# Forgetting attention with an MLP behind it: batch 1's loads issued in another order, five banks for the first scores, a bank of its own for the last pair's second head

## The chip, the cores and the metric

The kernel runs on one core of one Trainium2 chip. The metric is the time that the device takes for one execution, in microseconds (us), as the median of several runs; lower is better. A profile of one execution gives a trace. Its span runs from the first to the last instruction, and the execution's own time is a little longer than the span.

The core's engines work side by side, each through its own list of instructions in order: TensorE (PE: matmuls, and PEld for the loads of its weights), VectorE (DVE), ScalarE (ACT), GpSimd (POOL) and SyncE (SP). They wait for each other through semaphores. GpSimd and SyncE also issue DMAs, the transfers between the device's memory and the core; all of GpSimd's go through one queue.

## What is computed

There are 8 batches with 8 heads, 576 positions and 64 values per head. For each head, with `cum` the running sum of log f:

```python
scores = scale * np.matmul(q, k.transpose(0, 1, 3, 2))
log_f = np.log(np.clip(f, 0.0001, 1.0))
cum = np.cumsum(log_f, axis=-1)
decay = cum[:, :, :, None] - cum[:, :, None, :]
scores = np.where(causal, -1000000000.0, scores + decay)
attn = np.exp(scores - max) / (sum + 1e-09)
x = np.matmul(attn, v)
h = x @ w_in
out = (h - np.tanh(h)) @ w_out
```

The result of the attention, with the heads of a position side by side, is 4608 rows of 512 values. Each goes through an MLP with 2048 hidden values. Inputs and output are fp32; the kernel loads q, k, v and the weights as fp16.

## The kernel before

**Pairs.** The attention is done for two heads at a time: 32 pairs, four to a batch. Pairs are numbered from 0, so pairs 0 to 3 are batch 0 and pair 4 is the first of batch 1 (`NPAIR` is 4). For a pair, q and k are turned on TensorE into `QT` and `KT` (`trans`, two copies by VectorE or ScalarE each; from batch 3 on, transposing DMAs do this). Then come seven score tiles (`scores`, tiles 0 to 6; tile 3 holds the short last blocks of both heads). Each is a product into a PSUM bank, an exponential on ScalarE into a tile `e` (or `el`), and a causal mask. For pairs 0 to 3 (`early`) the mask is a small extra product on TensorE; from pair 4 on GpSimd cuts `e` (line 311). The pair's `values` multiply e with v, one pair later, and VectorE divides by the row sums into `xn`. `turn` transposes xn into `XR`, the MLP's input: on TensorE for batch 0, by two DMAs of SyncE for later ones.

**The decay** is added through three extra rows of QT and KT, filled by DMAs of SyncE from `cc` and `cqs`. These hold `cum`, which comes from a clip (line 160), a logarithm on ScalarE and a scan on VectorE. The very first head takes the decay by extra products instead, so that it need not wait for those DMAs.

**The MLP** works on nine blocks of 512 rows. A block has 16 steps `mlp1` (one 128-wide piece of the hidden layer each: four matmuls into `hps`, tanh `th` on ScalarE, sum `gt` on VectorE) and 16 steps `mlp2` (four matmuls each; every fourth ends a product `ops`, copied out and stored). `mlp1_part` does the first three matmuls of a step ahead ("h0" to "h2"), before the last pair of batch 0 is turned.

**What sets the order.** The program is written in the order in which each engine runs it. For pairs 0 to 4 `ORDERS` is a list by hand: "s" a score tile, "q" and "k" turns of a pair, "va" and "vb" the values of the two heads of the pair before, "x" its `turn`, "m" the next MLP step, "h" a part step, "r" rows and pads for the second buffers, and a number so many idle matmuls (`spin`) on a spare bank. From pair 5 on, a fixed count of MLP steps (`take`: 5 up to pair 8, then 8) is spread over each pair's items; so a step's place depends on how many are done before. `LOADS` says behind which score tile of which pair a load is issued: `(3, 3)` is behind pair 3's tile 3. Loads and masks share GpSimd's list, so a load behind a mask is issued when that mask is done, and a mask behind a load waits for the load to be issued.

**Banks.** PSUM has eight banks: two for scores (`ps_sc`), two for the values of a pair (`ps_av`, one for each head), one for turns (`ps_tr`), three for the MLP (`ps_m`; before the MLP starts, the turns of pairs 0 to 3 use them).

Of the kernel before, what the change touches and what calls it, by code (L numbers as in the profile page):

```python
# [14 lines left out]
PITCH = 640  # L15
# [7 lines left out]
def kernel(  # L23
# [111 lines left out]
    def load_aug(b, h0=0):  # L135
# [19 lines left out]
    nc.vector.memset(QT[0][D:D + 3, 0, :], 0.0)  # L155
    nc.vector.memset(KT[0][0:D, :, S:PITCH], 0.0)
    nc.vector.memset(KT[0][D:D + 3, 1:H, S:PITCH], 0.0)
    nc.vector.memset(neg16, 0.0)
    nc.vector.memset(tri16, 0.0)
    nc.vector.tensor_scalar(out=lf, in0=lf, scalar1=0.0001, scalar2=1.0,  # L160
                            op0=ALU.max, op1=ALU.min)
# [9 lines left out]
    nc.vector.memset(vn[0][D:P, NJ - 1, :, :], 0.0)  # L171
    nc.vector.memset(vn[0][:, :, :, D:VW], 1.0)
# [16 lines left out]

    def later_rows():  # L190
# [10 lines left out]
    def load_wout(t0, t1):  # L201
# [3 lines left out]
    QW = DFF // 4  # L205
    LOADS = {(0, 3): [lambda: load_win(0, QW), lambda: load_win(QW, 2 * QW)],
             (1, 3): [lambda: load_win(2 * QW, 3 * QW), lambda: load_win(3 * QW, DFF)],
             (2, 3): [lambda: load_qk(qn, q, 1, 0, 2), lambda: load_qk(kn, k, 1, 0, 2)],
             (3, 3): [lambda: load_wout(0, NFT // 2), lambda: load_qk(qn, q, 1, 2, 4),
                      lambda: load_qk(kn, k, 1, 2, 4), lambda: load_wout(NFT // 2, NFT)],  # L210
             (NPAIR, 1): [lambda: load_v(1)],
             (NPAIR, 4): [lambda: load_qk(qn, q, 1, 4, H), lambda: load_qk(kn, k, 1, 4, H),
                          lambda: const_rows(0, 0, 1)],
             (NPAIR, 6): [lambda: load_qk(qn, q, 2, 0, H), lambda: load_qk(kn, k, 2, 0, H)]}
# [18 lines left out]
    E, XN, AV, HP, GT, M2 = {}, {}, {}, {}, {}, {}  # L233

# [5 lines left out]
    def trans(b, c, src, dst, early, engs):  # L240
        pn, g3 = S // NT6, NT6 // 2
        if early:
            t32 = ps_m.tile([P, UW], FP32, tag="m", name="t32")
        else:
            t32 = ps_tr.tile([P, UW], FP32, tag="tr", name="t32")
        t16 = t32.bitcast(FP16)[:, 0:2 * S // 2].rearrange("p (a g n) -> p a g n", a=2, g=g3)
        for a in range(2):
            for g in range(g3):
                nc.tensor.transpose(out=t16[:, a, g, :], in_=src[b % 2][:, 2 * c + a, 2 * g:2 * g + 2, :],  # L249
                                    identity=id16[0:pn, 0:pn])  # L250
# [23 lines left out]
    def scores(b, c, ti, early):  # L274
        ps = ps_sc.tile([P, 512], FP32, tag="sc", name="ps")
# [38 lines left out]
    def values(b, c, heads=(0, 1), apart=False):  # L314
        if 0 in heads:
            av = ps_av.tile([P, 2, 512], FP32, tag="av", name="av")
            AV[(b, c)] = av[:, :, 0:NJ * (D + 1)].rearrange("p a (i d) -> p a i d", i=NJ)
        av = AV[(b, c)]
        for a in heads:
            for ib in range(NJ):  # L320
                for j in range(ib + 1):
                    nc.tensor.matmul(out=av[:, a, ib, :], lhsT=E.pop((b, c, a, j, ib)),  # L322
                                     rhs=vn[b % 2][:, j, 2 * c + a, 0:D + 1],
                                     start=(j == 0), stop=(j == ib))
        h0, hn = (heads[0], 1) if apart else (0, 2)
        if not apart and 1 not in heads:
            return
        if (b, c) not in XN:
# [3 lines left out]
        nc.vector.tensor_scalar_add(out=rs, in0=av[:, h0:h0 + hn, :, D:D + 1], scalar1=1e-9)  # L332
        nc.vector.reciprocal(out=rs, in_=rs)
        nc.vector.tensor_tensor(out=xn[:, :, h0 * D:(h0 + hn) * D].rearrange("p i (a d) -> p a i d", a=hn),  # L334
                                in0=av[:, h0:h0 + hn, :, 0:D],
# [17 lines left out]
    def mlp1_part(u, ft, c0, c1):  # L353
        if c0 == 0:
            HP[(u, ft)] = ps_m.tile([P, UW], FP32, tag="m", name="hps")
# [19 lines left out]
    def mlp2(u, s):  # L375
# [7 lines left out]
        if part == 3:  # L383
# [7 lines left out]
    BEGIN = ["8", "q0", "k0", "3", "s0", "q1", "s1", "k1", "s2", "s4", "s5", "q2", "r", "s6", "s3"]  # L391
    ORDERS = [BEGIN,
# [5 lines left out]

    def att_items(p):
# [12 lines left out]
        if p <= NPAIR:  # L412
            for what in ORDERS[p]:
# [6 lines left out]
                elif kind in "qk":  # L420
                    put(trans, *pairs[p + int(arg)], *((qn, QT) if kind == "q" else (kn, KT)), early,
# [5 lines left out]
                elif kind == "r":  # L427
                    put(later_rows)
                elif kind == "x":
# [75 lines left out]
```

## Time and profile before

| | |
|---|---|
| median of the timed runs | 369.54 us (369.54, 368.87, 371.0) |
| the profiled execution | 368.07 us |
| its span | 366.4 us |
| TensorE busy | 346.3 us, 95% |
| ScalarE busy | 219.2 us, 60% |
| VectorE busy | 183.1 us, 50% |
| GpSimd busy | 162.7 us, 44% |
| GpSimd's DMA queue | 18.36 MB, 75.3% of 16 engines' span |

The page cuts the span into 40 slices and gives each engine's busy share in tenths, and the clock that TensorE was granted. The other views are: the waits, summed by who waited for whom; the chain of work that ended last; the instructions in order of time (start, length, engine, line, operation, what it writes and reads; in brackets the idle time ahead of it and what ended it); and tables by stretches. In these the columns are the stretch, its length, the busy time and count of TensorE, PEld, VectorE, ScalarE and GpSimd, the granted clock, the DMA share and GB/s.

### The profile page before, as it was taken

The page shows a single profiled execution, that of the slowest core. Times are in us where ns is not written, and L with a number is a line of the kernel's source. Part 1 is how long each engine was busy: PE and PEld are TensorE (multiplying, and loading weights), DVE is VectorE, ACT ScalarE, POOL GpSimd, SP SyncE. Part 2 cuts the span into 40 slices and gives each one's busy share as a digit, 9 for nine tenths or more (in the row PEclk, how much of TensorE's full clock was granted, in tenths as well). Part 3 has the DMA queues.
Part 4 walks back from the last instruction along what each step waited for, and adds up shares of the span by engine and source line. Part 5 has one row for each costly group of instructions (what it writes and reads, how often), then busy time and mean ns, then how long its engine had stood idle before and what let it go on. Part 6 is the DMA issues. An engine that isn't in the chain of part 4 may idle for free.

```text
span 366.4 us, 7488 instructions
## 1 busy us (share of the span) xinstructions
PE 346.3 (95%) x2787; PEld 189.6 (52%) x2787; DVE 183.1 (50%) x358; ACT 219.2 (60%) x413; POOL 162.7 (44%) x318
## 2 busy tenths in 40 slices
PE   5986839999999999999999999999999999999995
PEld 2663415565555555555556875555555554444442
DVE  7564745445882278327832683278227622812710
ACT  5674644657865686568756875687568733623621
POOL 8950195587546754765476537662222210000000
PEclk9899997999999999999999999999999999999999
DMA  9999999999949994999399969994220022012002
GB/s 102 129 191 192 139 105 152 123 137 163 119 79 140 133 168 61 142 149 150 68 139 135 151 84 139 137 152 85 73 75 16 18 75 73 1 40 76 0 33 83
DMA packets 164819, 38.73 MB, mean 106 GB/s; under 512 B 155779, under 2 KB 160111, under 8 KB 164783
## 3 DMA queue, kind: packets, MB, share of 16 engines
q0 software_dynamic: 116480, 18.36, 75.3%
q1 hardware_dynamic: 48302, 19.90, 27.2%
q8 instruction: 22, 0.36, 0.4%
q14 instruction: 15, 0.11, 0.1%
HBM read 36.85 MB, written 9.44 MB: 126 GB/s over the span
## 4 chain that ended last, share of the span: by engine, by line
PE 89%; DVE 3%; ACT 2%; DMA 2%; POOL 1%; issue 1%; ACTq 0%
PE ops L381 33%; PE hps L363 33%; PE ps L287 12%; PE av L322 8%; ACT e L301 1%; DMA qn<-in_q_dram 1%; PE t L249 1%; DMA XR<-xn 1%; POOL vn L106 1%; DVE xn L334 1%; ACT th L370 1%; PE ps L295 0%; DVE gt L373 0%; DVE cum L173 0%; PE ps L290 0%
## 5 line engine op out<-in xcount | busy, mean ns | idle before, releaser
L373 DVE TENSOR_TENSOR gt<-hps,th 128x512 f16<-128x512 f32 x144 | 99.4, 691 | 92.8 <-ACT th L370 91.9
L363 PE MATMUL hps<-XR,win 128*128 128x512 f16 (+1 forms) x640 | 141.0, 359 | 1.7 <-DVE gt L373 1.0
L381 PE MATMUL ops<-wout,gt 128*128 128x512 f16 x576 | 139.1, 379 | 0.0
L301 ACT ACTIVATE e<-ps 128x512 f16<-128x512 f32 x192 | 110.4, 594 | 37.3 <-PE ps L287 31.1
L311 POOL TENSOR_SCALAR_AFFINE_SELECT e<-e 128x128 f16<-128x128 f16 x168 | 56.8, 340 | 125.0 <-ACT e L301 124.4
L370 ACT ACTIVATE th<-hps 128x512 f32<-128x512 f32 x144 | 86.1, 599 | 39.0 <-PE hps L363 38.2
L363 PEld LDWEIGHTS <-win 128*128 128x128 f16 x640 | 58.2, 98 | 50.7 <-issue 3.2
L287 PE MATMUL ps<-QT,KT 67*128 67x64 f16 (+4 forms) x384 | 78.6, 279 | 3.6 <-DVE KT L260 1.8
L381 PEld LDWEIGHTS <-gt 128*128 128x128 f16 x576 | 51.9, 97 | 52.4
L385 ACT ACTIVATE ost<-ops 128x512 f32<-128x512 f32 x36 | 21.5, 597 | 63.4 <-PE ops L381 49.1
L287 PEld LDWEIGHTS <-KT 67*128 67x128 f16 x384 | 36.8, 98 | 39.2 <-issue 4.2
L322 PEld LDWEIGHTS <-e 128*128 128x128 f16 x896 | 33.2, 98 | 8.0 <-issue 1.6
L322 PE MATMUL av<-vn,e 128*128 128x65 f16 x896 | 34.7, 194 | 1.0 <-DVE xn L334 1.0
L332 DVE TENSOR_SCALAR rs<-av 128x10 f32<-128x10 f32 (+1 forms) x33 | 5.4, 164 | 49.7 <-PE av L322 49.3
L106 POOL DMA_DIRECT2D vn<-in_v_dram x32 | 28.7, 899 | 3.0 <-PE hps L363 1.2
L334 DVE TENSOR_TENSOR xn<-av,rs 128x640 f16<-128x640 f32 (+1 forms) x33 | 26.6, 805 | 1.1
L87 POOL DMA_DIRECT2D qn<-in_q_dram x25 | 22.2, 889 | 1.3 <-issue 0.8
L87 POOL DMA_DIRECT2D kn<-in_k_dram x25 | 21.4, 857 | 1.3 <-issue 1.1
L260 DVE COPY QT<-t 64x576 f16<-64x576 f16 x22 | 9.9, 452 | 13.6 <-PE t L249 13.5
L260 DVE COPY KT<-t 64x576 f16<-64x576 f16 (+1 forms) x26 | 11.2, 429 | 4.3 <-PE t L249 4.1
L322 PE MATMUL av<-vn,el 128*128 128x65 f16 x64 | 12.4, 195 | 0.0
L249 PE MATMUL t<-id,qn 96*128 96x96 f16 x72 | 5.8, 224 | 5.8 <-DMA qn<-in_q_dram 5.8
(62 smaller groups left out, 134.6 us busy)
## 6 DMA issues: line engine op xcount, KB each, us to landing
out_dram<-ost SPq DMA_DIRECT2D x36, 256.0 KB
vn<-in_v_dram POOLq DMA_DIRECT2D x32, 128.0 KB, 4.9
qn<-in_q_dram POOLq DMA_DIRECT2D x20, 128.0 KB, 4.7
kn<-in_k_dram POOLq DMA_DIRECT2D x20, 128.0 KB, 4.4
win<-in_moe_w_in_dram POOLq DMA_DIRECT2D x4, 512.0 KB, 10.7
wout<-in_moe_w_out_dram POOLq DMA_DIRECT2D x2, 1024.0 KB, 18.9
XR<-xn SPq DMA_TRANSPOSE x56
qn<-in_q_dram POOLq DMA_DIRECT2D x6, 144.0 KB, 4.4
```

The costliest lines, as they stand in the source:

```text
L87: nc.gpsimd.dma_start(out=dst[b % 2][0:pn, n, :].rearrange("p (h d) -> p h d", h=H), in_=src[b, :, n * P:n * P + pn, :].rearrange("h p d - ...
L106: nc.gpsimd.dma_start(out=vn[b % 2][:, n, h0:h1, 0:D], in_=v[b, h0:h1, n * P:(n + 1) * P, :].rearrange("h p d -> p h d"))
L287: nc.tensor.matmul(out=ps[:, col:col + n], lhsT=KT[b % 2][0:D + 3, h, j * P:(j + 1) * P], rhs=QT[b % 2][0:D + 3, h, i0:i0 + n], start=True ...
L301: nc.scalar.activation(out=e[:, lo:hi], in_=ps[:, lo:hi], func=AF.Exp, scale=qscale)
L311: nc.gpsimd.affine_select(out=view, in_=view, compare_op=ALU.is_ge, fill=0.0, base=0, pattern=pat, channel_multiplier=-1)
L322: nc.tensor.matmul(out=av[:, a, ib, :], lhsT=E.pop((b, c, a, j, ib)), rhs=vn[b % 2][:, j, 2 * c + a, 0:D + 1], start=(j == 0), stop=(j == ib))
L334: nc.vector.tensor_tensor(out=xn[:, :, h0 * D:(h0 + hn) * D].rearrange("p i (a d) -> p a i d", a=hn), in0=av[:, h0:h0 + hn, :, 0:D], in1=r ...
L363: nc.tensor.matmul(out=hps[:, o:o + n], lhsT=win[:, ci, ft * P:(ft + 1) * P], rhs=XR[:, ci, t:t + n], start=(ci == 0), stop=(ci == NCH - 1))
L370: nc.scalar.activation(out=th, in_=hps, func=AF.Tanh, scale=-1.0)
L373: nc.vector.tensor_tensor(out=gt, in0=hps, in1=th, op=ALU.add)
L381: nc.tensor.matmul(out=ops, lhsT=GT[(u, ft)][:, m * P:(m + 1) * P], rhs=wout[:, ft, :], start=(ft == 0), stop=(ft == NFT - 1))
L385: nc.scalar.activation(out=ost, in_=ops, func=AF.Copy)
```

## The change

**Loads.** Batch 1's loads are put in another order and place. Before, q and k of heads 2 and 3 stood around w_out's halves behind pair 3's tile 3, v behind pair 4's tile 1, q and k of heads 4 to 7 behind pair 4's tile 4. Now all of them stand behind tiles 3 of pairs 2 and 3. Batch 2's k moves from pair 4 to pair 5. GpSimd's list, before, from the first load of batch 1's k on (`qn_92`, `kn_94`, `vn_96` are the buffers of batch 1; `qn_91`, `kn_93`, `vn_95` those of batch 2; L311, after the change L319, is the mask):

```order
L81 DMA kn_94<-in_k_dram 96x12x64
L202 DMA wout<-in_moe_w_out_dram 128x8x512
L81 DMA qn_92<-in_q_dram 96x12x64
L81 DMA kn_94<-in_k_dram 96x12x64
L202 DMA wout<-in_moe_w_out_dram 128x8x512
L311 AFFINE_SELECT e<-e 128x128 x2
L106 DMA vn_96<-in_v_dram 128x8x64 x4
L98 DMA vn_96<-in_v_dram 64x8x64
L311 AFFINE_SELECT e<-e 128x2x128
L311 AFFINE_SELECT el_116<-el_116 128x128
L311 AFFINE_SELECT e<-e 128x128
L81 DMA qn_92<-in_q_dram 96x24x64
```

The same place of GpSimd's list after the change:

```order
L81 DMA kn_94<-in_k_dram 96x12x64
L81 DMA qn_92<-in_q_dram 96x12x64
L81 DMA kn_94<-in_k_dram 96x12x64
L106 DMA vn_96<-in_v_dram 128x8x64 x4
L98 DMA vn_96<-in_v_dram 64x8x64
L204 DMA wout<-in_moe_w_out_dram 128x8x512 x2
L81 DMA qn_92<-in_q_dram 96x24x64
L81 DMA kn_94<-in_k_dram 96x24x64
L319 AFFINE_SELECT e<-e 128x128 x2
L319 AFFINE_SELECT e<-e 128x2x128
L319 AFFINE_SELECT el_116<-el_116 128x128
```

No load of batch 1 stands behind a mask any more, and v stands ahead of w_out.

**The start.** On VectorE the clip of log f moves ahead of the memsets of the mask constants, and four memsets of pads move behind the first turns ("p" in the list). VectorE's list before, from the first memset of KT on:

```order
L154 MEMSET KT_99 3x320
L155 MEMSET QT_97 3x288
L156 MEMSET KT_99 64x8x32
L157 MEMSET KT_99 3x7x32
L158 MEMSET neg_108 128x64
L159 MEMSET tri_109 128x64
L160 TENSOR_SCALAR lf<-lf 64x576
L171 MEMSET vn_95 64x264
L172 MEMSET vn_95 128x40x2
L173 TENSOR_SCALAR cum<-ones_110,lf 64x576
```

VectorE's list there after the change:

```order
L154 MEMSET KT_99 3x320
L155 TENSOR_SCALAR lf<-lf 64x576
L157 MEMSET neg_108 128x64
L158 MEMSET tri_109 128x64
L159 MEMSET QT_97 3x288
L169 TENSOR_SCALAR cum<-ones_110,lf 64x576
```

The scan (`cum`) has four memsets fewer ahead of it, and the clip five. On TensorE three spins ahead of the first score tile become five, the turn of pair 1's q, and four more.

**Banks.** In pairs 0 to 3 the score tiles go round five banks: the two of `ps_sc` and the three of `ps_m`. Turns keep the `ps_m` banks only in pair 0, without k of pair 1; later ones use `ps_tr`. The values of pair 3 use `ps_av` for head 0 and a bank of `ps_sc` for head 1. One more part step, "h3", takes a bank of `ps_sc`.

**The order by hand.** In pairs 1 to 3 the values come one score tile later. In pair 4 the part steps stand around the values, and fourteen MLP steps are done instead of thirteen. So every MLP step from pair 5 on stands one place earlier. ScalarE's list before, in pair 8, from the last exponential of tile 3 on (`th` is the first step of block 1, L385 `ost` the copy of the last product of block 0):

```order
L301 ACTIVATE el_115<-ps 128x128
L301 ACTIVATE e<-ps 128x512 x2
L385 ACTIVATE ost<-ops 128x512
L301 ACTIVATE e<-ps 128x512
L370 ACTIVATE th<-hps 128x512
```

ScalarE's list there after the change:

```order
L309 ACTIVATE el_115<-ps 128x128
L309 ACTIVATE e<-ps 128x512
L401 ACTIVATE ost<-ops 128x512
L309 ACTIVATE e<-ps 128x512
L386 ACTIVATE th<-hps 128x512
L309 ACTIVATE e<-ps 128x512
L386 ACTIVATE th<-hps 128x512
```

Block 1's first step now has a score tile of pair 8 behind it, and a second step follows in the same pair.

The diff, cut to its core:

```diff
@@ loads @@
-             (2, 3): [lambda: load_qk(qn, q, 1, 0, 2), lambda: load_qk(kn, k, 1, 0, 2)],
-             (3, 3): [lambda: load_wout(0, NFT // 2), lambda: load_qk(qn, q, 1, 2, 4),
-                      lambda: load_qk(kn, k, 1, 2, 4), lambda: load_wout(NFT // 2, NFT)],
-             (NPAIR, 1): [lambda: load_v(1)],
-             (NPAIR, 4): [lambda: load_qk(qn, q, 1, 4, H), lambda: load_qk(kn, k, 1, 4, H),
-                          lambda: const_rows(0, 0, 1)],
-             (NPAIR, 6): [lambda: load_qk(qn, q, 2, 0, H), lambda: load_qk(kn, k, 2, 0, H)]}
+             (2, 3): [lambda: load_qk(qn, q, 1, 0, 2), lambda: load_qk(kn, k, 1, 0, 2),
+                      lambda: load_qk(qn, q, 1, 2, 4), lambda: load_qk(kn, k, 1, 2, 4)],
+             (3, 3): [lambda: load_v(1), lambda: load_wout(0, NFT // 2), lambda: load_wout(NFT // 2, NFT),
+                      lambda: load_qk(qn, q, 1, 4, H), lambda: load_qk(kn, k, 1, 4, H)],
+             (NPAIR, 4): [lambda: const_rows(0, 0, 1)],
+             (NPAIR, 6): [lambda: load_qk(qn, q, 2, 0, H)],
+             (NPAIR + 1, 3): [lambda: load_qk(kn, k, 2, 0, H)]}
@@ banks: scores, values, the fourth part step @@
-        ps = ps_sc.tile([P, 512], FP32, tag="sc", name="ps")
+        if early and SEEN[0] % 5 > 1:
+            ps = ps_m.tile([P, 512], FP32, tag="m", name="ps")
+        else:
+            ps = ps_sc.tile([P, 512], FP32, tag="sc", name="ps")
+        SEEN[0] += 1
...
+        if apart and 1 in heads:
+            av = ps_sc.tile([P, 1, 512], FP32, tag="sc", name="av1")
...
+            if (u, ft) == (0, 3):
+                HP[(u, ft)] = ps_sc.tile([P, UW], FP32, tag="sc", name="hps")
+            else:
+                HP[(u, ft)] = ps_m.tile([P, UW], FP32, tag="m", name="hps")
@@ the order by hand @@
-    BEGIN = ["8", "q0", "k0", "3", "s0", "q1", "s1", "k1", "s2", "s4", "s5", "q2", "r", "s6", "s3"]
+    BEGIN = ["8", "q0", "k0", "5", "q1", "4", "s0", "s1", "k1", "p", "s2", "s4", "s5", "q2", "r", "s6", "s3"]
...
-              ["va", "vb", "h0", "h1", "h2", "x", "m", "m", "m", "m", "q0", "m", "k0", "m", "m", "m",
-               "s0", "m", "s1", "m", "q1", "s2", "m", "s3", "m", "k1", "s4", "s5", "m", "s6"]]
+              ["va", "h0", "vb", "h1", "h2", "h3", "x", "m", "m", "m", "m", "q0", "m", "m", "m", "k0", "m", "m",
+               "s0", "m", "s1", "m", "q1", "s2", "m", "s3", "m", "s4", "k1", "m", "s5", "s6"]]
```

More of the change, by code (lines that the diff above doesn't have):

```diff
@@ L154 @@
     nc.vector.memset(KT[0][D:D + 3, 0, :], 0.0)
-    nc.vector.memset(QT[0][D:D + 3, 0, :], 0.0)
-    nc.vector.memset(KT[0][0:D, :, S:PITCH], 0.0)
-    nc.vector.memset(KT[0][D:D + 3, 1:H, S:PITCH], 0.0)
+    nc.vector.tensor_scalar(out=lf, in0=lf, scalar1=0.0001, scalar2=1.0,
+                            op0=ALU.max, op1=ALU.min)
     nc.vector.memset(neg16, 0.0)
     nc.vector.memset(tri16, 0.0)
-    nc.vector.tensor_scalar(out=lf, in0=lf, scalar1=0.0001, scalar2=1.0,
-                            op0=ALU.max, op1=ALU.min)
+    nc.vector.memset(QT[0][D:D + 3, 0, :], 0.0)
     load_qk(qn, q, 0, 4, 6)
@@ L188, with pads @@
     load_qk(kn, k, 0, 6, H)
+    def pads():
+        nc.vector.memset(KT[0][0:D, :, S:PITCH], 0.0)
+        nc.vector.memset(KT[0][D:D + 3, 1:H, S:PITCH], 0.0)
+        nc.vector.memset(vn[0][D:P, NJ - 1, :, :], 0.0)
+        nc.vector.memset(vn[0][:, :, :, D:VW], 1.0)
     def later_rows():
@@ L238, in spin, with trans @@
             nc.tensor.matmul(out=t32, lhsT=ones16[:, 0:P], rhs=ones16[:, 0:UW])
[L240 removed]
+    def trans(b, c, src, dst, first, engs):
         pn, g3 = S // NT6, NT6 // 2
[L242 removed]
+        if first:
             t32 = ps_m.tile([P, UW], FP32, tag="m", name="t32")
@@ L314, in values @@
     def values(b, c, heads=(0, 1), apart=False):
-        if 0 in heads:
+        h0, hn = (heads[0], 1) if apart else (0, 2)
+        if apart and 1 in heads:
+            av = ps_sc.tile([P, 1, 512], FP32, tag="sc", name="av1")
+            AV[(b, c)] = av[:, :, 0:NJ * (D + 1)].rearrange("p a (i d) -> p a i d", i=NJ)
+        elif 0 in heads:
             av = ps_av.tile([P, 2, 512], FP32, tag="av", name="av")
@@ L318, in values @@
         av = AV[(b, c)]
+        if apart and 0 in heads:
+            av = av[:, 0:1]
         for a in heads:
@@ L321, in values @@
                 for j in range(ib + 1):
-                    nc.tensor.matmul(out=av[:, a, ib, :], lhsT=E.pop((b, c, a, j, ib)),
+                    nc.tensor.matmul(out=av[:, a - h0, ib, :], lhsT=E.pop((b, c, a, j, ib)),
                                      rhs=vn[b % 2][:, j, 2 * c + a, 0:D + 1],
                                      start=(j == 0), stop=(j == ib))
-        h0, hn = (heads[0], 1) if apart else (0, 2)
         if not apart and 1 not in heads:
@@ L420, in att_items @@
                 elif kind in "qk":
-                    put(trans, *pairs[p + int(arg)], *((qn, QT) if kind == "q" else (kn, KT)), early,
+                    put(trans, *pairs[p + int(arg)], *((qn, QT) if kind == "q" else (kn, KT)), p == 0 and what != "k1",
                         "VV" if p or arg != "0" else "AAAA" if kind == "q" else "VVVV")
@@ L428, in att_items @@
                     put(later_rows)
+                elif kind == "p":
+                    put(pads)
                 elif kind == "x":
```

9 lines of the change are left out of this document (4 added, 5 removed), and 6 rows, old and new, of the table ORDERS.

## The prediction

> **What bounds the kernel now.** I read the page first, for the engine that fills the span and where it has holes.
>
> ```profile
> PE 346.3 (95%) x2787; PEld 189.6 (52%) x2787; DVE 183.1 (50%) x358; ACT 219.2 (60%) x413; POOL 162.7 (44%) x318
> PE   5986839999999999999999999999999999999995
> PEclk9899997999999999999999999999999999999999
> ```
>
> TensorE is busy 95% of 366.4 us, and its holes lie in the first six slices of 9.2 us and in the last. After about 60 us only work taken off TensorE, or a new hole, can move the end. The view of waits names the largest hole, and a small one that matters below:
>
> ```profile
> PE t L249 <- DMA qn<-in_q_dram: 5.8, 1, 5.8
> PE hps L363 <- DMA XR<-xn: 0.2, 1, 0.2
> ```
>
> The table by stretches, cut at that hole, shows what it costs, and two stretches of other interest:
>
> ```profile
> 9.07:12.48 3.41, 3.41 (x21) 1.93 (x22) 1.41 (x4) 0.85 (x3) 3.41 (x5) 0.50 1.71 116
> 49.63:55.38 5.75, 0.00 (x0) 0.00 (x1) 0.50 (x1) 0.76 (x2) 5.75 (x9) 0.83 1.91 122
> 55.38:60.27 4.89, 4.89 (x44) 3.22 (x45) 1.97 (x5) 1.20 (x2) 3.55 (x5) 0.50 2.40 153
> 8.99:49.63 40.64, 34.19 (x365) 21.17 (x365) 25.34 (x57) 25.62 (x49) 19.33 (x29) 0.96 1.42 155
> ```
>
> The first number after the length is TensorE's busy time; the third from the end is the granted clock. From 49.63 to 55.38 TensorE does nothing, and then runs 4.89 us at clock 0.50, which wastes half of it, 2.4 us. The hole and its aftermath cost 5.75 + 2.4 = 8.2 us. Why the load is late is in the chain of waits:
>
> ```profile
> 45.12 2.02 POOL vn L106 x3
> 47.15 0.56 issue
> 47.70 0.90 POOL vn L106
> 48.60 0.69 POOL vn L98
> 49.29 0.43 POOL e L311
> ...
> 50.12 5.22 DMA qn<-in_q_dram
> 55.38 0.66 PE t L249 x6
> ```
>
> GpSimd issues the load of q for heads 4 to 7 of batch 1 only at 50.12, behind batch 1's v and the masks of the fifth pair (the change's "slot 4"). Its own rows show that it had stood idle long before:
>
> ```profile
> 14.91 3.04 POOL L198 DMA_DIRECT2D win<-in_moe_w_in_dram  x4
> 23.20 0.88 POOL L81 DMA_DIRECT2D kn<-in_k_dram  x1 [1.73 <-DMA win<-in_moe_w_in_dram]
> 25.75 0.89 POOL L202 DMA_DIRECT2D wout<-in_moe_w_out_dram  x1 [1.68 <-DMA win<-in_moe_w_in_dram]
> 43.75 0.29 POOL L311 TENSOR_SCALAR_AFFINE_SELECT e<-e 128x128 f16<-128x128 f16 x1 [17.12 <-ACT e L301]
> ```
>
> **The loads, the main term.** The new list issues q, k (heads 0 to 3), v, both halves of w_out, then q and k (heads 4 to 7) of batch 1 before the fifth pair's first mask. All go through GpSimd's one queue, so the late load now ends when the bytes ahead of it are through:
>
> ```profile
> DMA to landing us min/median/max: 18.5/18.9/19.4
> 25.00:28.00 3.00, 2.40 (x46) 1.87 (x44) 1.09 (x3) 2.61 (x6) 0.89 (x1) 1.00 1.24 207
> 49.00:51.00 2.00, 0.39 (x1) 0.10 (x1) 0.87 (x2) 1.39 (x3) 2.00 (x5) 1.00 2.26 144
> 53.00:62.00 9.00, 6.62 (x56) 4.09 (x57) 3.17 (x7) 2.19 (x5) 5.93 (x7) 0.62 2.43 151
> vn<-in_v_dram POOLq DMA_DIRECT2D x32, 128.0 KB, 4.9
> vn<-in_v_dram POOLq DMA_DIRECT2D x8, 64.0 KB, 4.6
> qn<-in_q_dram POOLq DMA_DIRECT2D x1, 288.0 KB, 5.2
> ```
>
> The first row is that of w_out's two loads. The second half was issued at 25.75 and so landed at 44.3 to 45.2, in the middle 44.7. Ahead of it in the new order stands v as well (4 x 128 + 64 = 576 KB), behind it the 288 KB of q: 864 KB, 885 thousand bytes, more than had passed by 44.7. The last number of the rows by stretches is GB/s: 207 while a weight streams, 144 to 151 while q, k and v do. The added bytes are of the second kind: 5.9 to 6.1 us, taken as 6.0. So q lands at about 50.8 (44.3 + 5.9 = 50.2 to 45.2 + 6.1 = 51.3) instead of 55.38: 4.6 us earlier (4.1 to 5.2).
>
> The Trainium skill ("DMA: Bandwidth & Descriptors", section "Anatomy of one DMA — SWDGE (gpsimd) path") fits one such load by 2.0 us plus its bytes at 436 thousand per us. By that rule the added bytes would take about 2 us, and the load would land near 47; the measured 144 to 207 GB/s contradict it, and the sum goes by them.
>
> The queue has to be fed for this. GpSimd's two waits above are on win: eight loads earlier in its list in each case, and the new list keeps that distance. Win's quarters landed at 23.2 and 25.75 and, 2.55 us apart, the others at 28.3 and 30.9; v's first four blocks follow them. The last issue (k, heads 4 to 7) waits for v's first block: after the 144 KB loads of q and k before it, four at 1 us (147 thousand bytes at 147 GB/s) from 30.9, plus 0.9, some 36. GpSimd is free by 37.5, before the masks, unless these come over 6 us sooner than 43.75. I cost it at nothing; the cover is that distance.
>
> **The work ahead of the hole.** Everything else that the diff changes in pairs 0 to 4 is hidden by the remaining wait: the clip of log f ahead of the memsets, the pads, nine spins for three, five banks for two, the later values, the second head's own bank. TensorE reached the load at 49.63, and between 8.99 and then it was idle 40.64 - 34.19 = 6.45 us and lost 1.7 us at clock 0.50 (3.41 us in the first row by stretches). The new order puts one more first-layer product (0.87 us, below) ahead of the hole. So it gets there between 49.63 + 0.9 = 50.5, with no gain at all, and 49.63 - 6.45 - 1.7 + 0.9 = 42.4. Both are before 50.8. I expect about 44 to 46, most of the idle time being waits on banks and on xn that the extra banks remove, and a hole of some 5 to 7 us still. If that cover were gone, each us saved in the head would count.
>
> The product moved ahead of the hole comes off the path behind it:
>
> ```profile
> 61.25 0.87 PE hps L363 x4
> ```
>
> That is 0.9 us gained (fourteen products there instead of thirteen).
>
> **The clock after the hole.** The two low stretches above last 3.4 us (9.07 to 12.48) and, from the 0.83 of 5.75 us, about 2 us within the hole and 4.89 after it, 6.8, twice 3.4. I take it that the clock is granted in steps of 3.4 us, and falls after a step with little work. What is lost after the hole depends on where in a step it ends: with a step left low in part, 0.9 to 1.7 us; if that step has too little work, one more, 1.7 to 2.6. Before it was 2.4, near the top. I take 2.0: 0.4 us gained. Bounds: 0.2 lost to 2.4 gained, the latter if the hole is too short to drop the clock.
>
> The Trainium skill ("TensorE: Matmul & The Clock Gate", section "What's actually happening") has the same step of 3413 ns and says that it runs freely and does not restart with a kernel. If it started with the kernel the steps would lie as before (50.03 to 53.44), the loss would be 1.3 and the gain 1.1; by the page it cannot be counted on, and no single trace here can show which holds.
>
> **What the moved product costs later.** From the sixth pair on, a fixed number of MLP steps goes with each pair, so all later steps sit one place earlier. The first product of token block 1 was the last of the ninth pair; it now stands one place sooner, behind tile 4. It needs batch 1's last rows of XR:
>
> ```profile
> 81.34 0.19 PE L322 MATMUL av<-vn,el 128*128 128x65 f16 x1
> 83.86 1.03 PE L381 MATMUL ops<-wout,gt 128*128 128x512 f16 x4
> 84.72 0.60 PE L287 MATMUL ps<-QT,KT 67*128 67x448 f16 x4
> 85.16 0.81 PE L363 MATMUL hps<-XR,win 128*128 128x512 f16 x3
> 86.13 0.38 PE L363 MATMUL hps<-XR,win 128*128 128x512 f16 x1 [0.16 <-DMA XR<-xn]
> 84.17 1.22 SPq L351 DMA_TRANSPOSE XR<-xn  x1
> ```
>
> The rows come 4.8 us after the values end (81.34 to 86.13), and the fourth matmul already waited 0.16. The place it moves to is one MLP step (83.86 to 84.72) and the last score tiles (84.72 to 85.16) sooner: 0.86 + 0.44 = 1.3 us of new wait, since the landing hangs on the values alone. In later batches there is room:
>
> ```profile
> 120.47 1.11 SPq L351 DMA_TRANSPOSE XR<-xn  x1
> 123.36 1.03 PE L363 MATMUL hps<-XR,win 128*128 128x512 f16 x4
> ```
>
> There the transpose lands at about 120.47 + (86.13 - 84.17) = 122.4 and the fourth matmul needs it at 123.36 + 3 x 0.21 = 124.0: 1.6 us, of which the new place takes 0.86 + 0.22, so nothing is lost.
>
> The loads of batch 2 follow in another order, with k one pair later. Their first uses:
>
> ```profile
> 72.02 0.42 PE L249 MATMUL t<-id,qn 96*128 96x96 f16 x6
> 76.27 0.42 PE L249 MATMUL t<-id,kn 96*128 96x96 f16 x6
> ```
>
> Behind q (50.8) and k (2.0 more) of batch 1 come q of batch 2 (589 thousand bytes, 4.0 us, to 56.8), three blocks of v (0.9 each) and k (4.0), to 63.5. With the uses 4.6 earlier, at 67.4 and 71.7, both keep over 8 us: nothing.
>
> **Sum.** 4.6 + 0.9 + 0.4 - 1.3 = 4.6 us off. The profiled execution took 368.07 us (span 366.4), so its like would take 363.5. The timed runs have a median of 369.54, 1.5 above it; against them I predict 365.0.
>
> **Rivals.** (1) The hole is shorter or closes: q, k and v move as fast as the weight did. At 207 GB/s the 885 thousand bytes take 4.3 us, q lands at 49.0, and the end comes 1.7 sooner, 363.3; with the clock kept as well, 361.3. Against it stand 144 to 151 in two separate stretches. The page's 436 thousand bytes per us would go further the same way.
>
> (2) The queue is not kept full, or its loads hold GpSimd. If the last issues wait until 43.75 and later, the masks of the fifth pair queue behind them and the values after the hole wait for them. Then q lands at 54 or later, 1.4 us are gained there at most, the 0.9 and the 1.3 nearly cancel, and the time is 369.5 - 1.4 - 0.9 + 1.3 = 368.5 to 370: no change. It speaks for it that GpSimd did wait twice for a landing; against it, that both waits were under 2 us and 18 us lie between its last issue and its first mask.
>
> (3) Slower: the shift by one step meets late XR rows in every batch. Six more blocks follow; if each landing is as late as its use was before, each costs up to 1.08, 6.5 in all, and the time is 365.0 + 6.5 = 371.5. It decides against the change from 4.6 / 6 = 0.8 us for each on. The 1.6 us of room at 124 speak against it; for it, only that the room shrinks to 0.5.
>
> **Chances.** The forecast 0.67 (its own range 363.5 to 367); rival 1 0.10; rival 2 0.14; rival 3 0.06; the rest, 0.03, is slower in ways I don't see. A run tells a change of 0.5%, 1.85 us, from none: faster takes the forecast's 0.67 less 0.01 at its slow end and rival 1, 0.76; within 0.5% most of rival 2 and that end, 0.14; slower rival 3, the rest and 0.01 of rival 2, 0.10. The range, 362.4 to 367.6, takes the forecast's case with the ends of its terms (4.1 to 5.2, -0.2 to 2.4) and half of rival 1.
>
> **What would show it.** Right: q's transposes of the sixth pair start at 50 to 51.5 with a wait of 4 to 8 us on the load; a stretch at clock 0.50 follows; the first product of block 1 waits about 1.4 us on XR; the clock stays at 1.00 from 9 to 12 us; GpSimd's loads are all issued by 38. Wrong: a start after 53 (rival 2), below 49.5 (rival 1), or waits on XR in the pairs from the thirteenth on (rival 3).

## The result, and the profile after

The changed kernel took 366.4 us (median of six runs, 365.31 to 368.12) against 370.3 us for the kernel before in its six runs (368.87 to 371.81). The ratio is 0.9899, with a 95% interval of 0.986 to 0.9937: faster by 1.0%, 3.9 us. The forecast was 365.0 (362.4 to 367.6).

The profiled execution of after is the slowest of its six, 368.12 us with a span of 366.4 us (by chance that of before's), and has four steps of low clock where the four faster runs have about two, so the 3.9 us are read from the medians and, below, from a second execution of each kernel. From the page of after:

```profile
PE   7879889998999999999999999999999999999995
PEclk9956999999999999999999999999999999999999
```

The hole in the sixth slice is gone (3 has become 8). What is new is a low clock in slices 3 and 4, about 18 to 37 us. The view of waits of after has no wait on batch 1's q any more. The wait on XR, 0.2 before, has grown, and four lines are new:

```profile
PE hps L379 <- DMA XR<-xn: 3.4, 4, 1.8
PE x L359 <- DVE QT L264: 1.7, 1, 1.7
PE av L336 <- DMA vn<-in_v_dram: 1.0, 1, 1.0
PE x L359 <- DVE KT L264: 1.0, 1, 1.0
PE av L336 <- POOL e L319: 0.9, 2, 0.7
```

GpSimd's instructions in order of time show its list kept as the change means it: every load of batch 1 is issued by 36.7, and the first mask follows 11 us later.

```profile
29.50 0.87 POOL L106 DMA_DIRECT2D vn<-in_v_dram  x1 [1.90 <-DMA win<-in_moe_w_in_dram]
34.39 1.18 POOL L81 DMA_DIRECT2D qn<-in_q_dram  x1 [0.51 <-DMA kn<-in_k_dram]
35.56 1.17 POOL L81 DMA_DIRECT2D kn<-in_k_dram  x1
47.72 0.29 POOL L319 TENSOR_SCALAR_AFFINE_SELECT e<-e 128x128 f16<-128x128 f16 x1 [10.99 <-ACT e L309]
```

The page's row of that load (its KB, then the time from issue to landing), the stretches of after, and TensorE's rows at the load's first use and at the first product of token block 1:

```profile
qn<-in_q_dram POOLq DMA_DIRECT2D x1, 288.0 KB, 15.5
```

```profile
9.12:53.96 44.84, 37.44 (x364) 24.06 (x363) 26.12 (x60) 25.61 (x49) 21.85 (x32) 0.85 1.66 160
16.29:19.70 3.41, 1.77 (x32) 1.30 (x31) 1.68 (x5) 1.19 (x2) 3.41 (x5) 0.96 1.41 172
19.70:33.35 13.65, 11.93 (x117) 9.05 (x117) 4.26 (x11) 6.57 (x13) 6.63 (x9) 0.51 1.76 184
53.96:62.00 8.04, 8.04 (x85) 4.82 (x84) 4.85 (x11) 5.47 (x12) 7.81 (x11) 1.00 1.29 83
```

```profile
20.11 0.71 PE L359 MATMUL x<-id,xn 128*128 128x128 f16 x5 [1.66 <-DVE QT L264]
27.02 0.71 PE L359 MATMUL x<-id,xn 128*128 128x128 f16 x5 [0.98 <-DVE KT L264]
53.96 0.42 PE L253 MATMUL t<-id,qn 96*128 96x96 f16 x6
84.30 0.38 PE L379 MATMUL hps<-XR,win 128*128 128x512 f16 x1 [1.78 <-DMA XR<-xn]
```

The load lands at 34.39 + 15.5 = 49.9, 5.5 us sooner than before. TensorE reaches it only at 53.96 and waits for nothing; it runs at full clock behind it. So the hole has closed from the other side as well: TensorE needs 44.84 us from the first scores to this place, where before needed 40.64 (8.99 to 49.63). Most of that lies in 19.70 to 33.35, four steps at half clock, which follow a step in which TensorE was busy 1.77 of 3.41 us. The two waits of 1.66 and 0.98 us on the copies of QT and KT lie at the edge of this stretch and within it. In turn the score tiles wait less than before (1.8 us on KT and 1.6 us on exponentials then, 0.4 and 0.7 now).

### The profile page after: what moved, and what is told of

The parts are those of the page before. It is cut to its first block, busy times and chain, and to the rows that moved or that the text cites. A ratio compares the mean times of both kernels' runs of the same rounds, so it can differ in the third digit from the quotient of the medians.

```text
span 366.4 us, 7499 instructions
## 1 busy us (share of the span) xinstructions
PE 348.4 (95%) x2793; PEld 191.7 (52%) x2793; DVE 181.6 (50%) x358; ACT 220.2 (60%) x413; POOL 160.9 (44%) x318
## 4 chain that ended last, share of the span: by engine, by line
PE 79%; DMA 7%; POOL 4%; issue 4%; DVE 3%; ACT 2%; SPq 0%; POOLq 0%; ACTq 0%
PE hps L379 32%; PE ops L397 29%; PE ps L295 10%; PE av L336 7%; DMA XR<-xn 4%; DMA vn<-in_v_dram 2%; POOL vn L106 1%; DVE gt L389 1%; DVE xn L347 1%; DMA out_dram<-ost 1%; POOL kn L81 1%; ACT th L386 1%; POOL e L319 1%; ACT ost L401 1%; PE x L359 1%
## 5 line engine op out<-in xcount | busy, mean ns | idle before, releaser
L319 POOL TENSOR_SCALAR_AFFINE_SELECT e<-e 128x128 f16<-128x128 f16 x168 | 56.1, 335 | 125.3 <-ACT e L309 125.0
L295 PEld LDWEIGHTS <-KT 67*128 67x128 f16 x384 | 37.7, 100 | 43.6 <-issue 7.8
L401 ACT ACTIVATE ost<-ops 128x512 f32<-128x512 f32 x36 | 21.5, 597 | 50.9 <-PE ops L397 41.9
L336 PEld LDWEIGHTS <-e 128*128 128x128 f16 x896 | 34.2, 100 | 9.1 <-POOL e L319 1.4
L336 PE MATMUL av<-vn,e 128*128 128x65 f16 x896 | 36.0, 196 | 2.0 <-DMA vn<-in_v_dram 1.0
L87 POOL DMA_DIRECT2D qn<-in_q_dram x25 | 21.4, 854 | 0.8 <-issue 0.6
L309 ACT ACTIVATE el<-ps 128x128 f16<-128x128 f32 x32 | 8.9, 278 | 3.8 <-PE ps L295 3.0
```

Of the source, the lines that this page charges most:

```text
L87: nc.gpsimd.dma_start(out=dst[b % 2][0:pn, n, :].rearrange("p (h d) -> p h d", h=H), in_=src[b, :, n * P:n * P + pn, :].rearrange("h p d - ...
L295: nc.tensor.matmul(out=ps[:, col:col + n], lhsT=KT[b % 2][0:D + 3, h, j * P:(j + 1) * P], rhs=QT[b % 2][0:D + 3, h, i0:i0 + n], start=True ...
L309: nc.scalar.activation(out=e[:, lo:hi], in_=ps[:, lo:hi], func=AF.Exp, scale=qscale)
L319: nc.gpsimd.affine_select(out=view, in_=view, compare_op=ALU.is_ge, fill=0.0, base=0, pattern=pat, channel_multiplier=-1)
L336: nc.tensor.matmul(out=av[:, a - h0, ib, :], lhsT=E.pop((b, c, a, j, ib)), rhs=vn[b % 2][:, j, 2 * c + a, 0:D + 1], start=(j == 0), stop=( ...
L401: nc.scalar.activation(out=ost, in_=ops, func=AF.Copy)
```

## Experiments

**E1: before, one more execution.** No edit. The question was whether the low clock at 9 to 12 us belongs to the kernel.

> The kernel before, once more, for its trace. Both theories: q of heads 4 to 7 lands at 55.4 us, the hole ahead of it is 5 to 6 us. Where the low stretches of the clock lie may differ from the first trace; if the steps run freely, their edges do not fall on 9.07, 12.48, 53.44 and 60.27 again.

It took 369.62 us, span 367.9. Stretches of this execution, and its row at the load:

```profile
9.00:50.11 41.11, 34.67 (x365) 21.41 (x365) 25.32 (x57) 25.60 (x49) 19.29 (x29) 1.00 1.39 154
56.01:63.50 7.49, 7.49 (x63) 4.61 (x64) 3.50 (x7) 2.89 (x7) 3.77 (x6) 0.65 2.99 150
56.01 0.66 PE L249 MATMUL t<-id,qn 96*128 96x96 f16 x6 [5.90 <-DMA qn<-in_q_dram]
```

The column of the clock reads 1.00 from 9.00 to 50.11, but it does not show every low stretch. One product of the first scores, with 512 columns, in E1, in before and in after:

```profile
9.82 0.63 PE L292 MATMUL ps<-cqs,pick 128*128 128x512 f16 x1
9.79 0.63 PE L292 MATMUL ps<-cqs,pick 128*128 128x512 f16 x1
9.56 0.38 PE L300 MATMUL ps<-cqs,pick 128*128 128x512 f16 x1
```

E1 is as slow there as before, where the column reads 0.50; so its low clock at 9 to 12 us is there as well, and it ends at about 13.4 instead of 12.5. It is not there in every execution: E3, with the same start, runs its first product of 512 columns in 0.39 us. Until the first low step that a trace lists, the column reads 1.00 also where the rows run at half speed. Behind the hole the clock is low from 54.4 to 61.3 (0.65 over 7.49 us: 2.6 us lost), in before from 53.4 to 60.3. The hole itself is the same, 5.90 us. Where the edges of the steps lie is no property of the kernel; the hole is.

**E2: after, repeated, with five rounds.** No edit.

> The changed kernel, once more. Its profiled execution had mean clock 0.981 and a span of 366.4, four of its other runs 0.991 and 363.6 to 365.1. Expected: a ratio of 0.99 to the kernel before; if the profile falls on a run at 0.991, the score tiles of pairs 1 to 3 run at full clock, TensorE reaches q's transposes of the sixth pair near 48 and waits there 1 to 3 us for the load at 49.9.

It took 364.82 us (363.84 to 367.87), ratio 0.9893 (0.9848 to 0.9938); before beside it, 368.81 in 17 runs. Its profiled execution, span 363.7, has two low steps in the head instead of four. From its waits:

```profile
PE hps L379 <- DMA XR<-xn: 2.3, 3, 1.2
PE x L359 <- DVE QT L264: 1.7, 1, 1.7
PE x L359 <- DVE KT L264: 1.5, 1, 1.5
PE av L336 <- POOL e L319: 0.9, 2, 0.7
```

TensorE reaches the sixth pair's turns at 52.34 (near 48 was expected), again with no wait on the load. Its first score tile starts at 10.59, in the first trace of after at 9.12. E1 and E2 can be set against each other: the turns 3.7 us sooner (56.01 - 52.34), no low clock behind them (2.6), one product moved ahead of them (0.9), less the waits on XR (2.3 - 0.9 = 1.4) and on masks (0.9). That makes 4.9; the spans differ by 4.2.

**E3: the new loads alone.** Before with the new list of loads and nothing else:

```diff
-             (2, 3): [q(1, 0:2), k(1, 0:2)],
-             (3, 3): [load_wout(first half), q(1, 2:4), k(1, 2:4), load_wout(second half)],
-             (NPAIR, 1): [load_v(1)],
-             (NPAIR, 4): [q(1, 4:8), k(1, 4:8), const_rows(0, 0, 1)],
-             (NPAIR, 6): [q(2, 0:8), k(2, 0:8)]
+             (2, 3): [q(1, 0:2), k(1, 0:2), q(1, 2:4), k(1, 2:4)],
+             (3, 3): [load_v(1), load_wout(both halves), q(1, 4:8), k(1, 4:8)],
+             (NPAIR, 4): [const_rows(0, 0, 1)],
+             (NPAIR, 6): [q(2, 0:8)],
+             (NPAIR + 1, 3): [k(2, 0:8)]
```

(`q(b, heads)` stands for `lambda: load_qk(qn, q, b, ...)`.)

> The kernel before with the new list of loads alone; order, banks and start as before, thirteen MLP steps in pair 4. Theory A (the gain is the load's): TensorE arrives at 49.6 as before, the load lands at about 50, the hole shrinks from 5.75 to under 1 us and the clock does not fall after it: 8 us less than before, ratio 0.978, faster than the whole change. Theory B (the gain is the head's: banks, start, order): within 0.5% of before, since the head is as it was.

364.81 us (362.92 to 368.32), ratio 0.9887 (0.9832 to 0.9942): the gain of the whole change. The row at the load, and the stretches of the hole and behind it:

```profile
50.94 0.66 PE L249 MATMUL t<-id,qn 96*128 96x96 f16 x6 [2.34 <-DMA qn<-in_q_dram]
```

```profile
47.83:51.24 3.41, 0.83 (x8) 0.40 (x7) 1.01 (x2) 1.52 (x3) 2.60 (x4) 0.92 2.12 138
51.24:54.65 3.41, 3.41 (x40) 2.08 (x38) 1.16 (x3) 1.20 (x2) 2.21 (x4) 0.58 1.83 117
```

The load lands at 50.9, as forecast (50.8). A hole of 2.34 us stays, and one low step behind it. The gain is less than the 2.2% expected by the theory that the loads are the cause, but it is as much as the whole change gains: as far as the intervals tell, the rest of the change adds nothing.

**E4: the rest of the change without the loads.** After with the old list of loads (the diff of E3 the other way round).

> The changed kernel with the old list of loads. Theory A: the hole ends at 55 again whatever the head does; the product moved ahead saves 0.9 and its wait on XR costs 1.5, ratio 0.998 to 1.005. Theory B: most of the gain stays, ratio 0.99.

371.93 us (368.77 to 374.26), ratio 1.0088 (1.0055 to 1.0121): slower than before, and above the 1.005 expected.

```profile
58.69 0.66 PE L253 MATMUL t<-id,qn 96*128 96x96 f16 x6 [5.78 <-DMA qn<-in_q_dram]
```

TensorE arrives at 52.9 and still waits 5.78 us, since the old list issues the load behind masks, which come later when the head is slower. The rest of the change costs about 3 us here. E3 and E4 together give 0.9887 x 1.0088 = 0.997, but after is at 0.99: the two parts don't add up. Part of the slow head lies, with the new loads, where E3 has its hole of 2.34 us.

**E5: the step moved back.** After with four MLP steps instead of five in the sixth pair, so that block 1's first product comes one place later again:

```diff
-            take = 5 if p <= 2 * NPAIR else 8
+            take = 4 if p == NPAIR + 1 else 5 if p <= 2 * NPAIR else 8
```

> The changed kernel with four MLP steps instead of five in pair 5, so that all later steps stand where they stood before. If the wait of the first product of block 1 (1.2 to 1.8 us on XR) comes from the shift by one step, it falls to 0.2 to 0.9, as in the two traces of before, and 1 us of the time goes with it (ratio to before 0.986 to 0.988, about as good as can be told). If it comes from later landings, it stays.

365.07 us (364.84 to 367.71), ratio 0.9893 (0.985 to 0.9936): no difference from E2 that the intervals can tell (0.986 to 0.988 was expected). In the trace the wait is smaller:

```profile
85.78 0.38 PE L379 MATMUL hps<-XR,win 128*128 128x512 f16 x1 [0.44 <-DMA XR<-xn]
PE av L336 <- POOL e L319: 1.8, 2, 1.1
```

The waits on XR fall from 2.3 us (E2) to 0.4, but the values of the sixth pair, now earlier by a step, wait 1.8 instead of 0.9 on its masks. So the wait on XR does come from the shift by one step, and about half of what giving the place back saves goes to the masks (3.2 us of both waits in E2, 2.2 here).

**E6: the banks undone.** After with the scores on two banks and the turns of pairs 0 to 3 on the MLP's banks, as before:

```diff
-        if early and SEEN[0] % 5 > 1:
-            ps = ps_m.tile([P, 512], FP32, tag="m", name="ps")
-        else:
-            ps = ps_sc.tile([P, 512], FP32, tag="sc", name="ps")
-        SEEN[0] += 1
+        ps = ps_sc.tile([P, 512], FP32, tag="sc", name="ps")
...
-                    put(trans, ..., p == 0 and what != "k1",
+                    put(trans, ..., early,
```

> The changed kernel with the banks of before in pairs 0 to 3: scores on two banks, turns on the MLP's three. Loads, start and order are the change's. Theory C (turns of q and k now share the one bank with the turn of xn, and this makes the head slower): the waits of 1.7 and 1.5 us ahead of the first two turns of xn go down to about 0.6 each, the clock has less reason to fall, TensorE reaches q's transposes of the sixth pair near 49.5 instead of 52.3 to 54, and the time is 2 to 3 us below the changed kernel's, ratio 0.982. Theory D (two banks for scores were the limit, as the change's five assume): the score tiles wait more, TensorE arrives later than 52.3, ratio above 0.99.

366.18 us (363.53 to 370.1). Two of the six runs, the profiled one among them, had a clock of 0.968; the ratio, 0.988 (0.9838 to 0.9922), is that of the four others, at 0.99 to 1.00. It can't be told from E2's 0.9893, and theory C's 0.982 lies outside its interval. From the trace, a wait and two stretches:

```profile
PE x L355 <- DVE xn L343: 1.0, 2, 0.6
9.00:12.41 3.41, 3.11 (x30) 1.92 (x28) 2.23 (x7) 1.93 (x4) 3.41 (x7) 1.00 2.08 142
12.41:15.83 3.42, 2.88 (x29) 1.93 (x28) 1.89 (x7) 2.90 (x6) 3.42 (x7) 0.84 2.13 132
```

The waits of the turns of xn on the copies of QT and KT (1.7 and 1.0 to 1.5 in after) are gone. That settles what they are: in pairs 1 to 3 the turns of q, k and xn share the one bank of `ps_tr` once the scores have the others. It does not show that they make the head slower. Without them this execution has seven low steps, and TensorE reaches the sixth pair's turns only at 56.32 (theory C: 49.5). The first of these steps begins within the second stretch, and in the two stretches together TensorE was idle for 0.84 us.

**E7: q and k ahead of w_out.** E3 with one line of the list in another order:

```diff
-             (3, 3): [load_v(1), load_wout(both halves), q(1, 4:8), k(1, 4:8)],
+             (3, 3): [load_v(1), q(1, 4:8), k(1, 4:8), load_wout(both halves)],
```

> The kernel before with the new list of loads, but q and k of heads 4 to 7 ahead of w_out's two halves. Theory A (after the change of loads the rest of the hole is w_out's 10 us on the queue): q lands near 41, TensorE finds it there at 48 to 50, no hole, no fall of the clock behind it, 2.3 + 1.1 us less than with the loads alone: ratio 0.979. Rival: w_out's second half now lands near 53, and if the second-layer products that begin at 56 have to wait for it, the gain is lost there and the ratio stays at 0.989.

362.03 us (360.59 to 364.92), ratio 0.981 (0.9768 to 0.9852): nearly twice E3's gain, with intervals that just overlap. TensorE's rows at the load, at the values of the sixth pair and at block 1's first product:

```profile
48.44 0.42 PE L249 MATMUL t<-id,qn 96*128 96x96 f16 x6
58.02 0.23 PE L322 MATMUL av<-vn,e 128*128 128x65 f16 x2 [0.28 <-POOL e L311]
58.94 0.80 PE L322 MATMUL av<-vn,e 128*128 128x65 f16 x12 [0.69 <-POOL e L311]
81.33 0.38 PE L363 MATMUL hps<-XR,win 128*128 128x512 f16 x1 [1.89 <-DMA XR<-xn]
```

The load no longer ends a wait, and w_out, a megabyte per half and first needed later, is nowhere waited for. The mask waits are those of after. They come with the new place of batch 2's loads, between the sixth pair's masks on GpSimd's list (E10).

**E8: the start of after, with the order of before.** The start of after (clip, pads, spins) and its own bank for the last pair's second head, but the other banks, the order of pairs 1 to 3 and thirteen steps in pair 4 as before; E7's loads; and batch 2's q and k issued behind w_out, ahead of all masks.

> What the runs so far point to: start of the changed kernel (clip first, spins, pads later), banks and order of pairs 1 to 3 of before, the second head's own bank, thirteen MLP steps in pair 4, q and k of heads 4 to 7 ahead of w_out, and batch 2's q and k behind it, ahead of every mask. Expected: no hole in the sixth pair, no wait of the values on masks near 62 (0.9 us in the runs with the new loads), a wait on XR of 0.2 to 0.9; the head as before or 1 to 2 us quicker; ratio 0.972 to 0.979.

360.4 us (359.03 to 362.79), ratio 0.9767 (0.9725 to 0.9809). Its row at the sixth pair's turns:

```profile
48.66 0.42 PE L252 MATMUL t<-id,qn 96*128 96x96 f16 x6
```

Its first score tile starts at 10.54, and it needs 38.1 us from there to the turns.

**E9: after's head on E7's loads.** After with E7's line, so that it differs from E7 in all that the change does beside the loads:

> After with one edit: q and k of heads 4 to 7 of batch 1 are issued ahead of both halves of w_out, as in e7. E7 (before's head with the same loads) gave a ratio of 0.981 and reached the sixth pair's turns at 48.4 us with no wait on the load. Theory A: in after the load is no longer what TensorE waits for (53.96 and 52.34 us, no wait), so landing it still earlier gives nothing; what is left is the slower head (waits of the turns of xn for the one bank of turns, values ahead of v, low clock). Then e9 is at after's ratio, 0.985 to 0.992, about 0.8% (3 us) slower than e7, and reaches those turns at 52 to 54. Theory B: the head of after is no slower, and only the phase of the clock's steps lay worse in its two profiled executions. Then e9 is at e7's ratio, 0.978 to 0.984, and reaches the turns at 48 to 50.

366.26 us (362.67 to 369.64), ratio 0.9907 (0.9871 to 0.9943), against E7's 0.981. Landing the load sooner gives after nothing; its head costs about 1%, 3.6 us. The stretches of E9 and its first score tile, then E7's:

```profile
9.00:52.74 43.74, 36.93 (x375) 23.62 (x374) 26.38 (x60) 25.31 (x49) 21.79 (x32) 0.92 1.85 164
17.06:20.48 3.42, 1.76 (x39) 1.39 (x36) 2.66 (x7) 1.73 (x4) 3.42 (x5) 1.00 1.18 178
20.48:23.89 3.41, 3.41 (x40) 2.74 (x37) 0.46 (x1) 1.81 (x4) 1.13 (x2) 0.54 1.24 202
11.06 0.38 PE L295 MATMUL ps<-QT,KT 67*128 67x512 f16 x1
```

```profile
9.00:48.44 39.44, 33.00 (x365) 20.52 (x366) 25.16 (x57) 25.44 (x49) 22.59 (x33) 1.00 2.10 162
8.99 0.61 PE L287 MATMUL ps<-QT,KT 67*128 67x512 f16 x1 [0.37 <-DVE KT L260]
```

E9 is at the turns 4.3 us later, 3.93 of it busy and only 0.37 idle (6.81 against 6.44). Of this, 2.1 us lie ahead of the first score tile: up to 11.06 E9 runs the rest of its nine spins and the turn of pair 1's q, in part at half speed. From the first score tile on it needs 41.7 us and E7 39.4, 2.2 more. There the waits are hardly longer in sum; they are put together. Around 17 to 20.5 us TensorE is busy 1.76 of 3.42 us, and the next stretch runs at clock 0.54, which loses 0.46 x 3.41 = 1.6 us. A second pair of stretches at 24 to 31 us does the same, and 0.87 is the product moved ahead. These terms make more than the 2.2; E7 has a slow start of its own (0.61 us for its first product, where E9 has 0.38), and the rest of the difference is not worked out.

By these few runs the low steps are the greater part of the cost: E9's two at clocks of 0.999 and 0.998 took 362.7 and 362.8 us, E7's two at 0.999 and 1.00 took 360.6 and 362.1. And the start is not what costs: E8 has it too, with banks and order of before, and is at the turns at 48.66. From the first score tile on E8 needs 38.1 us and E9 41.7; 0.87 of these 3.6 us is the moved product. (Batch 2's loads, which E8 moves too, change nothing up to the turns: E7 reaches them at 48.44, E10 at 48.47.) That leaves 2.7 us to the banks and the order of pairs 1 to 4 together. E6 undid the banks alone and gained nothing that was measured; the order of before with the banks of after was not run, so which of the two it takes is open.

**E10: E7 with batch 2's loads ahead of the masks.** E7's list with `q(2, 0:8), k(2, 0:8)` behind w_out:

```diff
-             (3, 3): [load_v(1), q(1, 4:8), k(1, 4:8), load_wout(both halves)],
-             (NPAIR, 4): [const_rows(0, 0, 1)],
-             (NPAIR, 6): [q(2, 0:8)],
-             (NPAIR + 1, 3): [k(2, 0:8)]
+             (3, 3): [load_v(1), q(1, 4:8), k(1, 4:8), load_wout(both halves),
+                      q(2, 0:8), k(2, 0:8)],
+             (NPAIR, 4): [const_rows(0, 0, 1)]
```

> E7 (before with the new loads, q and k of heads 4 to 7 ahead of w_out) with one edit: batch 2's q and k are issued behind w_out, ahead of all masks, so that none of them stands between two masks. E7's values waited 0.28 + 0.69 us on the masks of the sixth pair and its turns 0.83 on k of batch 2. Theory A: these waits cost what they show. Then the mask waits are gone, those on batch 2's k too, w_out and v keep their places, and the time is 1 to 1.8 us under e7: a ratio of 0.976 to 0.979. Theory B: TensorE's next wait takes their place, or the longer queue holds GpSimd's masks. Then the ratio stays at 0.981 or rises, and the masks are late by more than before.

360.4 us (359.38 to 361.49), ratio 0.977 (0.9724 to 0.9815), 1.6 us under E7; the intervals of the two overlap. The first lines of its waits:

```profile
PE spin L237 <- DVE ones L142: 1.7, 1, 1.7
PE ps L286 <- ACT e L300: 1.6, 5, 0.5
PE t L248 <- DVE QT L259: 1.2, 1, 1.2
```

No wait on masks is left in the list, and those on XR come to 0.6 us. This is before with another list of loads and nothing else, 2.3% faster than before and 1.3% faster than after. E8, with the start of after and the extra bank of its last pair, comes to the same 360.4, so they add nothing that was measured.

## Why the prediction came out

The total was near: 365.0 forecast, 366.4 measured in one set of runs and 364.8 in the other. Its steps were partly right, and that the total lies in the range is in part luck, since errors of opposite sign met. From the trace of before to that of E2, in us: 3.0 sooner at the turns (4.6 forecast), 0.9 for the product, 2.4 for the clock behind the hole (0.4 forecast), less 2.1 on XR (1.3 forecast) and 0.9 on masks (nothing forecast). That makes 3.3 against the 4.6 forecast; the spans differ by 2.7.

**Where the load lands: right.** Forecast 50.8, measured 49.9 in after, 50.9 in E3. The sum by bytes and measured rates held. One stretch of after, w_out's tail, and the time after the last load of batch 1:

```profile
36.50:44.00 7.50, 6.26 (x41) 3.06 (x40) 4.90 (x10) 3.47 (x6) 0.23 (x1) 1.00 1.26 206
50.00:52.00 2.00, 2.00 (x18) 1.04 (x17) 1.93 (x5) 1.58 (x5) 0.70 (x2) 1.00 0.28 14
```

206 GB/s again for a weight; by 52 us the queue stands almost empty, as nothing more is issued before the masks.

The Trainium skill ("DMA: Bandwidth & Descriptors", section "Anatomy of one DMA — SWDGE (gpsimd) path") would by its 436 thousand bytes per us have put the landing near 47, an estimate; the trace has 49.9 and does not agree.

**GpSimd's list: right.** All loads of batch 1 issued by 36.7 (38 forecast), with waits of 0.4 to 1.9 us on earlier landings, and 11 us to the first mask. Rival 2 did not happen.

**The work ahead of the hole: wrong, the step that failed.** I put every edit of pairs 0 to 4 at nothing, since the hole would cover it, and expected TensorE at 44 to 46, sooner than before, because "the extra banks remove" its waits. It came at 53.96, 52.34 and 52.74, outside even the bounds of 42.4 to 50.5. Two things that I had put at nothing are in the rows. The nine spins for three, run in part at half speed, put off the first score tile from 8.99 to 10.59 (E2) and 11.06 (E9), though to no more than 9.12 in the first trace of after; E8 wins this back later. And between the first score tile and the turns E2 and E9 need 41.7 us, E7 and E10 39.4 to 39.5. There the extra banks for scores were taken from the turns, which now queue for one bank (E6), the waits bunch, and the clock is low for two to four steps (E9). That the waits bring the low clock is not shown: E6 has none of them and a low clock all the same in two of its six runs, and the later values of pairs 1 to 3 are a rival that no run tries alone. What E8 and E9 do show is that banks and order together cost some 2.7 us.

The forecast hole of 5 to 7 us was therefore none. E3, which has before's head, has 2.34 us, as TensorE came there at 48.6 and not at 44 to 46; its hole ends 4.4 us sooner than in the trace of before (50.94 against 55.38), close to the 4.6 forecast.

**The clock after the hole: wrong in place.** With no hole it does not fall there at all, a gain of 2.4 instead of 0.4. The loss has moved to the head: 13.65 us at 0.51 in the first profiled execution, two steps in E2 and E9.

**The moved product: right in size, but not all.** The 0.9 us lie ahead of the turns, where, without a hole, they cost what they save. The wait on XR was forecast at 1.4; it was 1.78, 1.23 (E2) and 1.31 (E9). In later batches I forecast none, and three more are there in after:

```profile
122.87 0.38 PE L379 MATMUL hps<-XR,win 128*128 128x512 f16 x1 [0.34 <-DMA XR<-xn]
160.36 0.38 PE L379 MATMUL hps<-XR,win 128*128 128x512 f16 x1 [0.47 <-DMA XR<-xn]
235.27 0.38 PE L379 MATMUL hps<-XR,win 128*128 128x512 f16 x1 [0.76 <-DMA XR<-xn]
```

They make 1.6 us (1.0 in E2, 1.4 in E9, each in two batches): rival 3 in part, in three batches of six and with 0.3 to 0.8 each instead of 1.08. The room of 1.6 us that I read at 124 us in the trace of before was short there by 0.3 after all, and I had read one batch for all. E5, which gives the place back in the sixth pair, has none of the three, but longer waits on the masks.

**Missed.** Batch 2's loads, put between the sixth pair's masks, hold these up: about 0.95 us of TensorE in after, E2, E3, E7 and E9, gone in E10. I had followed those loads along their queue and to their first uses, but not what stands behind them on GpSimd. The values of the first pair also came to v before it had landed (0.98 us in the profiled execution).

**Rival 1** (the hole closes, 361.3 to 363.3) named what was seen, but not why: not a faster load, but a later TensorE. What it forecast for the time needs both a closed hole and an unchanged head, which is E7: 362.0.

## What to carry to other kernels

A hole covers the work ahead of it only as long as it stays; when an edit closes the hole and slows the work ahead of it, price that work as if the hole were gone. Banks given to one use are taken from another: list what else takes turns on the bank that stays (here waits of 1.0 to 1.7 us; what they cost in time is not shown). And for each load that is moved, look at what is queued behind it on the engine that issues it; here a better order of the loads alone (first what is needed first, the weights behind, nothing between masks) gave 2.3%, and the rest of the change gave about 1% back.

## What was not expected of the hardware

TensorE's clock falls in steps of 3.41 us after a step with about half of the time idle, and not only after a hole: busy 1.77 of 3.41 (after), 1.76 of 3.42 (E9), and in E7 behind the wait on XR:

```profile
78.47:81.88 3.41, 1.52 (x12) 0.72 (x11) 0.00 (x0) 1.68 (x4) 2.38 (x5) 1.00 2.96 138
81.88:85.29 3.41, 3.41 (x16) 1.43 (x14) 2.17 (x4) 2.03 (x4) 1.31 (x3) 0.51 1.53 209
```

So 1.9 us of waiting cost another 1.6 there, or nothing: after's wait of 1.78 at the same place left the clock at 1.00. It depends on how the steps lie. Of the 16 falls in the first 100 us of the traces, 14 follow a step with 1.9 us of work or less; the two others, in E6 and E8, follow steps with 2.95 and 2.87, so busy time alone does not decide. Runs of one kernel with fewer low steps are faster: E9's two at clock 0.999 and 0.998 took 362.7 and 362.8 us, its nine around 0.991 took 365.1 to 366.8, and its one at 0.977 took 369.6.

The Trainium skill ("TensorE: Matmul & The Clock Gate", section "What's actually happening") says that these windows of 3413 ns run freely, and that the clock comes back after one busy window. The traces agree on the first: the low steps behind the hole begin at 54.4 in E1 and at 53.4 in before. On the second they agree if busy means full. In the first 100 us of the traces, all 14 low steps in which TensorE was busy 3.40 us or more were the last of their stretch; of the 19 with less, 17 were followed by another low step. The four of after (19.43 to 33.08) were busy 2.75, 3.19, 2.65 and 3.34 us, with the clock back behind the fourth. So short waits in a low stretch go with a clock that stays low. Why two came back without being full (the other is E3's, at about 3.2) is open; no run here varies this alone.
